# Window attention and a max-of-three feed-forward: later units' scores made with keys stationary, masked as 32x32 blocks, two pairs ahead

## The chip, the cores and the metric

The kernel runs on one core of a Trainium2 chip. The metric is the time of one execution in device microseconds (us). Engines are named as in the profile: PE (TensorE, the matmuls), PEld (TensorE's weight loads), DVE (VectorE), ACT (ScalarE), POOL (GpSimd) and SP (SyncE, whose queue issues the DMAs).

## The reference

Attention over 8 batches, 8 heads, 576 positions and 64 dimensions, then a feed-forward over all 4608 tokens with the maximum of three products:

```python
rel = pos[:, None] - pos[None, :]
mask_plain = (rel >= 0) & (rel < 32)
mask_dil = (rel >= 0) & (rel < 128) & (rel % 4 == 0)     # heads 4 to 7
scores = np.where(mask, q @ k.T / 8, -1e9)
attn = np.exp(scores - scores.max(-1)); attn /= attn.sum(-1) + 1e-9
x = (attn @ v)                                           # as tokens x 512
h = np.maximum(np.maximum(x @ w1, x @ w2), x @ w3)       # 512 -> 768
out = h @ w_out                                          # 768 -> 512
```

All of it is float32. A query sees 32 keys: its own and the 31 before it, in dilated heads those of its own residue modulo 4.

## The kernel before

**Units.** Attention is cut into 64 units: a unit `u` is two heads of one half (288 positions) of a batch; units 0 and 1 of each four are plain heads, 2 and 3 dilated ones. A plain unit has three blocks of 96 queries with 128 keys each, a dilated one four blocks (one residue each) of 72 queries with 104 keys. In a half that begins a sequence (`hf` 0) the first 32 keys of a block don't exist and are left out of the scores.

Units 0 to 11 (below `LEAN`) go through `dense`; their mask is added by a matmul, and their weights of attention are turned by PE (L590). Units 12 to 63 go through `attention` and `behind`, two at a time. For each block and head the scores are a matmul with the queries stationary and the keys streamed (L670): scores come out with queries on partitions. Per block and head, VectorE then adds the mask, scales and takes the maximum in one custom instruction (L702), ScalarE makes the exponential and its sum (L693); where `hf` is 0, POOL clears the missing columns (L728). POOL adds 1e-9 (L738), VectorE takes the reciprocal (L743), POOL multiplies, one instruction for each head (L750), and VectorE turns the result with six transposes of 32x32 blocks, those of the band only (L764), into `PT`. Two units' products with the values (L776, `pv`) follow, and ACT and VectorE round them into the halves `xH` and `xL` that the feed-forward reads.

**Feed-forward.** Nine tiles of 512 tokens. Each has 18 groups of 12 matmuls up (L828: three terms of four, from `wupH`, `wupL`, `xH`, `xL`) in one of two PSUM buffers, whose maximum VectorE keeps in `tmp`, and then four groups of 18 matmuls down (L883). The weights arrive packed and are unpacked on the chip in the start: byte extraction on POOL or VectorE (L420), two joining steps on VectorE (L424, L432), a cast (`wupH`), and a subtraction mostly on POOL (`wupL`, through the helper at L353).

**Order.** Everything is a step of `Plan`. `Plan.order` sets the order of each engine's queue by planned costs, ready times, due times (`deadlines`) and free buffers (`room`), and the program is issued in that order; nothing is reordered at run time. A pair's steps on PE are one step, `products`: the values of the pair that is ready, and behind them the scores of the next pair, so scores run one pair ahead of the values (`unit_pair`, L926). The scores use PSUM buffers "b", six of one bank each; a unit takes two of them for its scores, one for each head, and one for `pv`. While PE has nothing to do in the start, filler matmuls (L962) stand in its queue.

Of the kernel before, what the change touches and what calls it, by code (L numbers as in the profile page):

```python
# [18 lines left out]
WIN, DIL = 32, 4  # L19
# [4 lines left out]
NF = DF // 128  # L24
BLOCK = 256
# [23 lines left out]
def blocks_of(hf, dil):  # L49

    nb, nq, wk = (4, 72, 104) if dil else (3, 96, 128)
    step, out = (104 if dil else 96), []
    for i in range(nb):

        mo = WIN if not hf and (dil or i == 0) else 0
        out.append((nq * i, nq, HALF + step * i + mo, wk - mo, mo))
    return out


def columns(dil):  # L60

    return HALF + (4 * 104 if dil else 320)


class Buf:


    def __init__(self, pool, tag, limit, shape, dtype, name):
        self.pool, self.tag, self.limit = pool, tag, limit
        self.shape, self.dtype, self.name = shape, dtype, name  # L70
        self.users = 0
        self.number = None
        self.end = 0.0
        self.slot = None
        self.t = None

    def take(self):
        if self.t is None and isinstance(self.pool, list):
            self.t = self.pool[self.slot]
        elif self.t is None:  # L80
            self.t = self.pool.tile(self.shape, self.dtype, tag=self.tag, name=self.name, bufs=self.limit)
# [15 lines left out]
class Plan:  # L97
# [48 lines left out]
    def room(self, st, slots):  # L146

        new = [b.tag for b in st.bufs if b.slot is None]
        at = 0.0
        for b in st.bufs:  # L150
            if b.slot is None and b.number is not None and b.number >= self.given.get(b.tag, 0) + new.count(b.tag):
                return 1e9
        for tag in set(new):
            k = new.count(tag)
            at = max(at, sorted(slots[tag])[k - 1][0] if len(slots[tag]) >= k else 1e9)
        return at

    def order(self, fill=None):
# [13 lines left out]
        while len(order) - fills < len(self.steps):  # L172
# [21 lines left out]
            at, _, e, st = best  # L194
            if e == "pe" and st.kind == "ffn":
                fill = None
# [11 lines left out]
            assert at < 1e9, "the steps wait for each other's buffers"  # L208
            for b in st.bufs:
                if b.slot is None:  # L210
                    free_slot = min(slots[b.tag])
                    b.slot = free_slot[1]
                    slots[b.tag].remove(free_slot)
                    self.given[b.tag] = self.given.get(b.tag, 0) + 1
# [21 lines left out]
            for b in st.bufs:  # L236
                b.users -= 1
                b.end = max(b.end, end)
                if not b.users:
                    slots[b.tag].append((b.end + 0.2, b.slot))  # L240
# [21 lines left out]
def tile_dilated_window_attention__then__maxout_ffn(  # L262
# [27 lines left out]
    mask = masks[:, 1]  # L290
# [12 lines left out]
        "k": (4, [128, HALF + 416], F32),  # L303
# [14 lines left out]
    BANKS = {"b": 6, "ffn": 2}  # L318

    def buf(tag, name, shape=None, dtype=None):  # L320
        if tag in BANKS:
            return Buf(ps, tag, BANKS[tag], [128, 512], F32, name)
# [3 lines left out]
        return Buf(work, tag, n, shape or sh, dtype or dt, name)  # L326

# [12 lines left out]

    for t in KEPT["W"]:
        nc.gpsimd.memset(t[:, 768:], 0.0)

    def copy(eng, dst, src):
        if eng == "act":
            nc.scalar.copy(dst, src)  # L346
        elif eng == "pool":
            nc.gpsimd.tensor_scalar(dst, src, 1.0, 1.0, ALU.mult, ALU.mult)
        else:
            nc.vector.tensor_copy(dst, src)  # L350
# [105 lines left out]
    def loads(u, after):  # L456
# [16 lines left out]
            [kload, after[1]],  # L473
# [176 lines left out]
    def attention(u, after):  # L650
# [4 lines left out]
        blocks = blocks_of(hf, dil)  # L655
        nb, nq = len(blocks), blocks[0][1]
        wk = 104 if dil else 128
        kb, kload, v, vload = loads(u, after)
        W, mx, sm = buf("W", f"W{u}"), buf("mx", f"mx{u}"), buf("sm", f"sm{u}")
        banks = [buf("b", f"s{u}_{j}") for j in range(2)]  # L660

        def W3(c0=0):
            return W.t[:, c0 : c0 + 2 * nb * wk].rearrange("p (n k) -> p n k", k=wk)

        def scores():

            for i, (q0, _, k0, nk, mo) in enumerate(blocks):
                for j in range(2):
                    d = slice(64 * j, 64 * j + 64)
                    nc.tensor.matmul(  # L670
                        banks[j].t[:nq, wk * i : wk * i + nk],
                        kb.t[d, q0 : q0 + nq],
                        kb.t[d, k0 : k0 + nk],
                        start=True,
                        stop=True,
                    )

        cost = sum(x[3] / 600 + 0.01 for x in blocks)
        return (scores, cost, [kload], [kb, mx, W, *banks]), (
            lambda s: behind(u, s, blocks, banks, W, W3, mx, sm, v, vload)  # L680
        ), (kload, vload)

    def behind(u, s, blocks, banks, W, W3, mx, sm, v, vload):
# [3 lines left out]
        nb, nq = len(blocks), blocks[0][1]  # L687
        wk = 104 if dil else 128
        expd, cleared = [], None

        def expo(_, n, nk, mo):
            a = W3()[:nq, n, mo : mo + nk]
# [4 lines left out]
        for j in range(2):  # L697
            for i, (*_, nk, mo) in enumerate(blocks):
                n = nb * j + i

                def masked(_, n=n, i=i, j=j, nk=nk, mo=mo):
                    nc.vector.tensor_tensor_reduce(  # L702
                        W3()[:nq, n, mo : mo + nk],
                        banks[j].t[:nq, wk * i : wk * i + nk],
                        mask[:nq, mo : mo + nk],
                        -0.125,
                        3e38,
                        ALU.add,
                        ALU.min,
                        mx.t[:nq, n : n + 1],  # L710
                    )

                t = plan.add({"dve": dve(nk)}, masked, [s], [banks[j], W, mx])
                expd.append(
                    plan.add(
                        {"act": act(nk) + 0.33},
                        lambda _, n=n, nk=nk, mo=mo: expo(_, n, nk, mo),
                        [t],
                        [W, mx, sm],
                    )  # L720
                )


        if not hf:

            def clear(_):
                a = W3() if dil else W.t[:, :768].rearrange("p (j c) -> p j c", j=2)
                nc.gpsimd.memset(a[:, :, :WIN], 0.0)  # L728

            cleared = plan.add({"pool": 0.1 + 0.0008 * (256 if dil else 64)}, clear, [expd[0]], [W])  # L730

        PT = buf(f"PT{dil}", f"PT{u}")
        copied = []

        def eps(e):
            a = sm.t[:nq, : 2 * nb]
            if e == "pool":
                nc.gpsimd.tensor_tensor(a, a, eps_c[:nq].broadcast_to([nq, 2 * nb]), op=ALU.add)  # L738
            else:
                nc.vector.tensor_scalar(a, a, 1e-9, None, ALU.add)  # L740
# [3 lines left out]

        s = plan.add({"pool": 0.22}, eps, expd, [sm])
        r = plan.add({"dve": 0.18}, recip, [s], [sm])
        k0 = WIN if dil and not hf else 0
        normed = []
        for j in range(2):
            n0, n1 = j * nb, (j + 1) * nb  # L750

            def norm(e, n0=n0, n1=n1):
                a = W3()[:nq, n0:n1, k0:]
                tt(e, a, a, sm.t[:nq, n0:n1].unsqueeze(2).broadcast_to([nq, nb, wk - k0]), ALU.mult)

            n = nb * (wk - k0)
            normed.append(plan.add({"pool": 0.13 + 0.00188 * n, "dve": dve(n)}, norm, [r, cleared], [W, sm]))
        for i in range(3):
            for g in (i, i + 1):

                def turn(_, i=i, g=g):
                    c = 32 * g
                    e = max(0, c + 32 - wk)
                    nc.vector.transpose(  # L764
                        PT.t[c : c + 32, : 2 * nb, 32 * i : 32 * i + 32],
                        W3(e)[32 * i : 32 * i + 32, :, c - e : c - e + 32],
                    )

                copied.append(plan.add({"dve": dve(64 * nb)}, turn, normed, [W, PT]))
# [3 lines left out]
        def values():  # L773
            for i, (q0, *_) in enumerate(blocks):
# [151 lines left out]
    def unit_pair(u):  # L926
# [8 lines left out]
        s, xs = products([x for _, x in made], [x[1] for x in pair])  # L935
        for (x, _), r in zip(made, xs):
            x_of[divmod(x, NPAIR)] = r(waits(x // NPAIR))
        made = [(x, rest(s)) for x, _, rest in pair]

    u = t0 = 0  # L940
    for n in TILES:
        plan.kind = "a"
        while HALF * (u // NPAIR) < t0 + n:

            for p in range(NPAIR):
# [3 lines left out]
                elif u == LEAN and p == 0:  # L949
                    unit_pair(u)  # L950
                if u >= LEAN and p % 2:
                    unit_pair(u + 1)
# [17 lines left out]
def _layouts(q, k, v, moe_w1, moe_w2, moe_w3, moe_w_out):  # L970
# [13 lines left out]
    for hf in range(2):  # L984
# [4 lines left out]
        lay[f"qk_d{hf}"] = np.concatenate(x, axis=2).transpose(0, 1, 3, 2).reshape(B, 2, 128, -1)  # L989
# [34 lines left out]
```

## Time and profile before

| | us |
|---|---|
| median of 3 runs | 723.75 (721.61 to 724.37) |
| profiled execution, its own time | 724.2 |
| its span, first to last instruction | 722.3 |

The page lists busy time by engine, the granted clock of PE in 40 slices, and groups of instructions with busy time (overlaps counted once) and the mean duration of one. Two groups that the prediction doesn't show: ScalarE's exponentials (L693) are 134.1 us busy in 364 instructions, and the feed-forward's four groups of 648 matmuls on PE are 676.6 us busy. The mean granted clock is 0.990.

### The profile page before, as it was taken

What the parts mean: (1) busy time and instruction counts of PE and PEld (TensorE: products, weight loads), DVE (VectorE), ACT (ScalarE), POOL (GpSimd) and SP (SyncE); (2) the same over time, 40 slices, a digit from 0 to 9 for tenths busy, and PEclk for the clock granted to TensorE, in tenths of its full rate; (3) what the DMA queues carried; (4) which work ended last, traced back from release to release, by engine and by line L of the source; (5) the groups of instructions that cost most, each with busy time, mean ns of one, the idle gap of its engine ahead of it and who ended that gap; (6) DMA issues with size and microseconds to landing.
All of it is one profiled execution on the core that took longest, in us unless ns stands there. A gap on an engine that the chain in (4) does not pass through costs nothing.

```text
span 722.3 us, 12780 instructions
## 1 busy us (share of the span) xinstructions
PE 712.2 (99%) x4534; PEld 578.2 (80%) x4539; DVE 371.7 (51%) x1456; ACT 294.5 (41%) x1101; POOL 231.9 (32%) x328
## 2 busy tenths in 40 slices
PE   8899999999999999999999999999999999999997
PEld 4577878888888888888888888888888888888886
DVE  5978966556556554655456555655555511101110
ACT  4866763334444444444434334434343411111111
POOL 3888762233223332322222222332223301200110
PEclk9969999999999999999999999999999999999999
DMA  8991532211222223212321222112220010000001
GB/s 262 344 325 49 185 101 93 75 32 58 89 89 63 59 78 102 63 59 64 103 77 60 63 76 92 49 37 80 87 64 25 15 44 0 1 29 30 1 0 59
DMA packets 31232, 57.45 MB, mean 80 GB/s; under 512 B 3008, under 2 KB 11200, under 8 KB 31168
## 3 DMA queue, kind: packets, MB, share of 16 engines
q1 hardware_dynamic: 31168, 56.64, 24.4%
q8 instruction: 36, 0.59, 0.3%
q14 instruction: 28, 0.23, 0.1%
HBM read 47.19 MB, written 9.44 MB: 78 GB/s over the span
## 4 chain that ended last, share of the span: by engine, by line
PE 95%; POOL 2%; DVE 1%; DMA 1%; issue 0%; SPq 0%; ACT 0%; POOLq 0%; ACTq 0%; DVEq 0%
PE u L828 62%; PE d L883 21%; PE s L670 5%; PE pv L776 4%; PE s L509 1%; DMA st<-in_w_up_dram 1%; POOL W L353 1%; PE pt L590 1%; PE pv L604 1%; PE idle L962 0%; POOL wupL L353 0%; PE s L504 0%; DVE mx L527 0%; DVE sm L544 0%; POOL c L420 0%
## 5 line engine op out<-in xcount | busy, mean ns | idle before, releaser
L353 DVE TENSOR_TENSOR tmp<-u,tmp 128x512 f32<-128x512 f32 x108 | 74.7, 691 | 206.6 <-PE u L828 190.0
L828 PE MATMUL u<-xL,wupH 128*128 128x512 f32 x648 | 176.3, 394 | 0.0
L828 PE MATMUL u<-xH,wupH 128*128 128x512 f32 x648 | 175.4, 393 | 0.0
L828 PE MATMUL u<-xH,wupL 128*128 128x512 f32 x648 | 174.1, 390 | 0.0
L883 PE MATMUL d<-wdn,h 128*128 128x512 f32 x648 | 150.8, 391 | 0.0
L353 POOL TENSOR_TENSOR h<-tmp,h 128x512 fp32r<-128x512 f32 x54 | 69.7, 1290 | 244.6 <-ACT h L346 244.6
L693 ACT ACTIVATE W<-W,mx 96x128 f32<-96x128 f32 (+3 forms) x364 | 134.1, 371 | 27.0 <-DVE mx L702 25.9
L828 PEld LDWEIGHTS u<-xH,wupL 128*128 128x128 f32 x648 | 121.4, 188 | 25.9
L883 PEld LDWEIGHTS d<-wdn,h 128*128 128x128 f32 x648 | 121.1, 188 | 26.3
L828 PEld LDWEIGHTS u<-xH,wupH 128*128 128x128 f32 x648 | 121.4, 189 | 25.8
L828 PEld LDWEIGHTS u<-xL,wupH 128*128 128x128 f32 x648 | 120.9, 189 | 26.4
L764 DVE STREAM_TRANSPOSE PT<-W 32x192 f32<-32x192 f32 (+1 forms) x312 | 124.7, 400 | 32.3 <-POOL W L353 28.1
L346 ACT CAST h<-tmp 128x512 fp32r<-128x512 f32 x54 | 33.4, 619 | 208.9 <-DVE tmp L353 208.8
L353 POOL TENSOR_TENSOR W<-W,sm 96x384 f32<-96x384 f32 (+3 forms) x125 | 99.2, 812 | 45.2 <-DVE sm L743 40.3
L702 DVE CUSTOM_DVE_ANT_0 W<-s,masks 96x128 f32<-96x128 f32 (+3 forms) x364 | 70.1, 257 | 52.6 <-PE s L670 52.6
L693 ACT ACTIVATION_READ_ACCUMULATOR W<-W,mx 72x1 f32 (+1 forms) x364 | 68.6, 189 | 0.0
L738 POOL TENSOR_TENSOR sm<-sm,small_c 96x6 f32<-96x6 f32 (+1 forms) x52 | 10.3, 198 | 166.3 <-ACT W L693 166.1
L346 ACT COPY tmp<-u 128x512 f32<-128x512 f32 x54 | 31.7, 587 | 67.9 <-PE u L828 51.2
L346 ACT COPY o<-d 128x512 f32<-128x512 f32 x36 | 21.1, 587 | 82.3 <-PE d L883 75.3
L670 PE MATMUL s<-k 64*96 64x128 f32 (+3 forms) x728 | 38.7, 254 | 0.0
L670 PEld LDWEIGHTS s<-k 64*72 64x72 f32 (+1 forms) x728 | 33.7, 149 | 2.8 <-ACT tmp L346 0.4
L776 PEld LDWEIGHTS pv<-PT,v 104*64 104x64 f32 (+1 forms) x728 | 27.2, 137 | 9.2 <-issue 8.8
(56 smaller groups left out, 410.9 us busy)
## 6 DMA issues: line engine op xcount, KB each, us to landing
k<-in_qk_d_dram SPq DMA_DIRECT2D x32, 352.0 KB, 3.0
k<-in_qk_p_dram SPq DMA_DIRECT2D x32, 304.0 KB, 3.2
st<-in_w_up_dram SPq DMA_DIRECT2D x18, 512.0 KB, 10.4
out_dram<-o SPq DMA_DIRECT2D x36, 256.0 KB, 2.0
v<-in_v_d_dram SPq DMA_DIRECT2D x32, 208.0 KB
v<-in_v_p_dram SPq DMA_DIRECT2D x32, 192.0 KB, 6.1
st<-in_w_dn_dram SPq DMA_DIRECT2D x12, 256.0 KB, 2.6
```

The costliest lines, as they stand in the source:

```text
L346: nc.scalar.copy(dst, src)
L353: (nc.vector if eng == "dve" else nc.gpsimd).tensor_tensor(dst, a, b, op=op)
L509: nc.tensor.matmul(S3(j)[:nq, i], kb.t[d, nq * i : nq * i + nq], kb.t[d, k0 : k0 + wk], start=False, stop=True, skip_group_check=True,)
L590: nc.tensor.transpose(bank.t[:wk, nq * i : nq * i + nq], W3()[:nq, nb * j + i], ident[:nq, :nq])
L670: nc.tensor.matmul(banks[j].t[:nq, wk * i : wk * i + nk], kb.t[d, q0 : q0 + nq], kb.t[d, k0 : k0 + nk], start=True, stop=True,)
L693: nc.scalar.activation(a, a, AF.Exp, bias=mx.t[:nq, n : n + 1], scale=-1.0, accum_out=sm.t[:nq, n : n + 1])
L702: nc.vector.tensor_tensor_reduce(W3()[:nq, n, mo : mo + nk], banks[j].t[:nq, wk * i : wk * i + nk], mask[:nq, mo : mo + nk], -0.125, 3e38, ...
L738: nc.gpsimd.tensor_tensor(a, a, eps_c[:nq].broadcast_to([nq, 2 * nb]), op=ALU.add)
L764: nc.vector.transpose(PT.t[c : c + 32, : 2 * nb, 32 * i : 32 * i + 32], W3(e)[32 * i : 32 * i + 32, :, c - e : c - e + 32],)
L776: nc.tensor.matmul(pv.t[64 * j : 64 * j + 64, q0 : q0 + nq], v.t[:wk, j, i, :], PT.t[:wk, nb * j + i, :nq], start=True, stop=True,)
L828: nc.tensor.matmul(sums(bank), wt[:, 3 * f + g, c, :], moving(xL if xz else xH, c), start=(m == 0 and c == 0), stop=(m == 2 and c == 3),)
L883: nc.tensor.matmul(bank.t, hs[f].t[:, hz, s0 : s0 + 128], wdn[f].t[:, wz], start=(f == 0 and m == 0), stop=(f == NF - 1 and m == 2),)
```

## The change

Scores of units 12 to 63 are made with the keys stationary (128 columns) and the queries streamed (96 or 72 columns; the last block streams 96 in every unit, for which the dilated loads are 24 columns longer), so that keys are on partitions. Both heads' scores lie in two neighbouring PSUM banks (`span=2`; the six banks "b" are now one tile). VectorE turns them back with six transposes of 32x32 blocks, of the band only, into `W`, which then holds 64 columns for each block and head instead of 128 or 104. The mask (`narrow`, bf16) is added by POOL, VectorE takes one maximum over all blocks, POOL scales it, the exponentials read 64 columns, and one multiplication on POOL normalises both heads. No columns are cleared any more. Scores run two pairs ahead of the values (`AHEAD`). In the dense units, the values' load no longer waits for the keys' load.

```diff
             lambda _: nc.sync.dma_start(out=v.t[:nk, :, :nb, :], in_=vsrc),
-            [kload, after[1]],
+            [after[1]] if u < LEAN else [kload, after[1]],
...
-            for i, (q0, _, k0, nk, mo) in enumerate(blocks):
+            for i in range(nb):
+                k0 = HALF + k_step * i
+                n = 96 if i == nb - 1 else nq
                 for j in range(2):
                     d = slice(64 * j, 64 * j + 64)
                     nc.tensor.matmul(
-                        banks[j].t[:nq, wk * i : wk * i + nk],
-                        kb.t[d, q0 : q0 + nq],
-                        kb.t[d, k0 : k0 + nk],
+                        sT.t[:, j, nq * i : nq * i + n],
+                        kb.t[d, k0 : k0 + 128],
+                        kb.t[d, nq * i : nq * i + n],
...
+        for i in range(3):
+            for g in range(2):
+                def turn_in(_, i=i, g=g):
+                    r = slice(32 * i, 32 * i + 32)
+                    c = 32 * (i + g)
+                    src = sT.t[c : c + 32, :, 32 * i : 32 * i + nq * (nb - 1) + 32]
+                    src = bass.AP(
+                        src.tensor, src.offset, [list(src.ap[0]), list(src.ap[1]), [nq * src.ap[2][0], nb], [src.ap[2][0], 32]]
+                    )
+                    dst = W3(r)[:, :, 32 * g : 32 * g + 32].rearrange("p (j n) k -> p j n k", j=2)
+                    nc.vector.transpose(dst, src)
+                turned.append(plan.add({"dve": dve(64 * nb)}, turn_in, [s], [sT, W]))
...
-                    nc.vector.tensor_tensor_reduce(
-                        W3()[:nq, n, mo : mo + nk],
-                        banks[j].t[:nq, wk * i : wk * i + nk],
-                        mask[:nq, mo : mo + nk],
...
+        t = plan.add({"pool": pool(nw)}, masked, turned, [W])
+        t = plan.add({"dve": dve(nw)}, most, [t], [W, mx])
+        t = plan.add({"pool": 0.22}, eighth, [t], [mx])
...
-                a, a, AF.Exp, bias=mx.t[:nq, n : n + 1], scale=-1.0, accum_out=sm.t[:nq, n : n + 1]
+                a, a, AF.Exp, bias=mx.t[:nq, n : n + 1], scale=0.125, accum_out=sm.t[:nq, n : n + 1]
...
+        s = plan.add({"pool": 0.13 + 0.00188 * nw, "dve": dve2(2 * nw)}, norm, [s], [W, sm])
...
-        s, xs = products([x for _, x in made], [x[1] for x in pair])
+        ready = made.pop(0) if len(made) == AHEAD else []
+        s, xs = products([x for _, x in ready], [x[1] for x in pair])
...
-        made = [(x, rest(s)) for x, _, rest in pair]
+        made.append([(x, rest(s)) for x, _, rest in pair])
```

PE's queue at the values of units 18 and 19 (`pv18`, `pv19`), in the second feed-forward tile, before; `s20_0` and `s20_1` are the scores of unit 20's two heads, `k20` its queries and keys, and the size is that of the output:

```order
L776 MATMUL pv18_1974<-PT1_0_86,v18_1632 64x72 x8
L776 MATMUL pv19_1975<-PT1_1_87,v19_1670 64x72 x8
L670 MATMUL s20_0_1977<-k20_1626 96x128
L670 MATMUL s20_1_1978<-k20_1626 96x128
L670 MATMUL s20_0_1977<-k20_1626 96x128
L670 MATMUL s20_1_1978<-k20_1626 96x128
L670 MATMUL s20_0_1977<-k20_1626 96x128
L670 MATMUL s20_1_1978<-k20_1626 96x128
```

The same place in the changed kernel, where all scores and values lie in the tile `banks`:

```order
L794 MATMUL banks_89<-PT1_0_87,v18_1631 64x72 x8
L794 MATMUL banks_89<-PT1_1_88,v19_1658 64x72 x8
L690 MATMUL banks_89<-k22_1625 128x72 x6
L690 MATMUL banks_89<-k22_1625 128x96 x2
L690 MATMUL banks_89<-k23_1655 128x72 x6
L690 MATMUL banks_89<-k23_1655 128x96 x2
```

Behind the values of 18 and 19 now stand the scores of 22 and 23, not of 20 and 21, and the outputs have 128 partitions of keys and 72 or 96 columns of queries. Both programs have 364 such matmuls.

SP's queue in the start before, from the third key load to the third packed weight (`st2`); `k` are queries and keys, `v` values:

```order
L465 DMA k2_106<-in_qk_d0_dram 128x704
L465 DMA k3_108<-in_qk_d0_dram 128x704
L438 DMA st0_110<-in_w_up_dram 128x512
L438 DMA st1_112<-in_w_up_dram 128x512
L472 DMA v0_133<-in_v_p0_dram 128x2x192
L465 DMA k4_147<-in_qk_p1_dram 128x608
L465 DMA k5_167<-in_qk_p1_dram 128x608
L472 DMA v1_173<-in_v_p0_dram 128x2x192
L465 DMA k6_177<-in_qk_d1_dram 128x704
L472 DMA v2_204<-in_v_d0_dram 104x512
L472 DMA v3_209<-in_v_d0_dram 104x512
L438 DMA st2_217<-in_w_up_dram 128x512
```

And in the changed kernel, again up to `st2`:

```order
L495 DMA v1_118<-in_v_p0_dram 128x2x192
L495 DMA v5_120<-in_v_p1_dram 128x2x192
L495 DMA v2_139<-in_v_d0_dram 104x512
L495 DMA v3_141<-in_v_d0_dram 104x512
L495 DMA v4_143<-in_v_p1_dram 128x2x192
L488 DMA k4_155<-in_qk_p1_dram 128x608
L488 DMA k5_171<-in_qk_p1_dram 128x608
L461 DMA st0_179<-in_w_up_dram 128x512
L488 DMA k6_203<-in_qk_d1_dram 128x728
L461 DMA st1_210<-in_w_up_dram 128x512
L488 DMA k7_231<-in_qk_d1_dram 128x728
L461 DMA st2_243<-in_w_up_dram 128x512
```

The six value loads `v0` to `v5` and the key loads `k4` and `k5` moved ahead of the first weight, `st0` (`v0` stands two rows ahead of the first one shown, right behind `k2`).

POOL's queue in the start before, up to the last normalisation (`W<-W,sm`) that the first feed-forward tile needs, that of unit 7 (`W_80`):

```order
L353 TENSOR_TENSOR W_81<-W_81,sm_406 96x384 x2
L353 TENSOR_TENSOR W_83<-W_83,sm_316 96x416 x2
L353 TENSOR_TENSOR wupL<-c_313,wupH 128x512
L353 TENSOR_TENSOR wupL<-c_385,wupH 128x512
L353 TENSOR_TENSOR W_82<-W_82,sm_446 96x416 x2
L420 TENSOR_SCALAR c_567<-st_336 128x512
L420 TENSOR_SCALAR c_595<-st_356 128x512
L353 TENSOR_TENSOR W_80<-W_80,sm_562 96x416 x2
```

And in the changed kernel, up to the same normalisation (`W_81` there):

```order
L376 TENSOR_TENSOR W_82<-W_82,sm_376 96x384 x2
L376 TENSOR_TENSOR W_84<-W_84,sm_312 96x416 x2
L376 TENSOR_TENSOR wupL<-c_289,wupH 128x512
L376 TENSOR_TENSOR W_83<-W_83,sm_406 96x416 x2
L443 TENSOR_SCALAR c_525<-st_292 128x512
L376 TENSOR_TENSOR W_81<-W_81,sm_492 96x416 x2
```

From the queue's head to this row there were seven byte extractions (`c<-st`) and four subtractions (`wupL`); now there are five and two, and one cast to `wupH`.

More of the change, by code (lines that the diff above doesn't have):

```diff
@@ L24 @@
 NF = DF // 128
+PAD = 24
+AHEAD = 2
 BLOCK = 256
@@ L46, with __init__ @@
 WEIGHT_PACE, WEIGHT_SLACK, WEIGHT_LEAD = 0.3, 3.188, 0.8
[L49 to L57, printed above, removed]
 def columns(dil):
-    return HALF + (4 * 104 if dil else 320)
+    return HALF + (4 * 104 + PAD if dil else 320)
 class Buf:
-    def __init__(self, pool, tag, limit, shape, dtype, name):
+    def __init__(self, pool, tag, limit, shape, dtype, name, span=1):
+        self.span = span
         self.pool, self.tag, self.limit = pool, tag, limit
@@ L194, in order @@
             at, _, e, st = best
+            assert at < 1e9, "the steps wait for each other's buffers"
             if e == "pe" and st.kind == "ffn":
@@ L207, in order @@
                 fills += 1
-            assert at < 1e9, "the steps wait for each other's buffers"
-            for b in st.bufs:
+            self.now = at
+            for b in sorted(st.bufs, key=lambda b: -b.span):
                 if b.slot is None:
-                    free_slot = min(slots[b.tag])
-                    b.slot = free_slot[1]
-                    slots[b.tag].remove(free_slot)
+                    b.slot = self.pick(b, slots[b.tag])
                     self.given[b.tag] = self.given.get(b.tag, 0) + 1
@@ L239, in order @@
                 if not b.users:
-                    slots[b.tag].append((b.end + 0.2, b.slot))
+                    slots[b.tag] += [(b.end + 0.2, b.slot + i) for i in range(b.span)]
             for n in st.next:
@@ L289, in tile_dilated_window_attention__then__maxout_ffn @@
     masks = const.tile([128, 4, 128], BF16, name="masks")
-    mask = masks[:, 1]
+    narrow = const.tile([96, 4, 64], BF16, name="narrow")
     wupH = const.tile([128, 3 * NF, 4, 128], F32R, name="wupH")
@@ L316, in tile_dilated_window_attention__then__maxout_ffn, with buf @@
     }
[L318 to L322, printed above, removed]
+    NB = 6
+    banks_b = ps.tile([128, NB, 512], F32, name="banks", bufs=1)
+    BANKS = [banks_b[:, i] for i in range(NB)] + [banks_b[:, i : i + 2] for i in range(0, NB, 2)]
+    def buf(tag, name, shape=None, dtype=None, span=1):
+        if tag == "b":
+            return Buf(BANKS, tag, NB, None, None, name, span)
+        if tag == "ffn":
+            return Buf(ps, tag, 2, [128, 512], F32, name)
         if tag in KEPT:
@@ L676, in scores, with behind @@
                     )
-        cost = sum(x[3] / 600 + 0.01 for x in blocks)
-        return (scores, cost, [kload], [kb, mx, W, *banks]), (
-            lambda s: behind(u, s, blocks, banks, W, W3, mx, sm, v, vload)
+        cost = nb * (nq / 600 + 0.03) + 0.03
+        return (scores, cost, [kload], [kb, mx, W, sT]), (
+            lambda s: behind(u, s, nb, nq, sT, W, mx, sm, v, vload)
         ), (kload, vload)
-    def behind(u, s, blocks, banks, W, W3, mx, sm, v, vload):
+    def behind(u, s, nb, nq, sT, W, mx, sm, v, vload):
         half, p = divmod(u, NPAIR)
@@ L745, in behind @@
         s = plan.add({"pool": 0.22}, eps, expd, [sm])
[L746 to L757, printed above, removed]
+        s = plan.add({"dve": 0.18}, recip, [s], [sm])
```

137 lines of the change are left out of this document (77 added, 60 removed).

## The prediction

> **What bounds the kernel now.** I read the page first: busy time of each engine, and the chain of work that ended last.
>
> ```profile
> PE 712.2 (99%) x4534; PEld 578.2 (80%) x4539; DVE 371.7 (51%) x1456; ACT 294.5 (41%) x1101; POOL 231.9 (32%) x328
> PE 95%; POOL 2%; DVE 1%; DMA 1%; issue 0%; SPq 0%; ACT 0%; POOLq 0%; ACTq 0%; DVEq 0%
> ```
>
> TensorE is busy for 99% of the span, and the chain runs through it for 95%. A busy PE need not be a PE at its peak, so the next views are its waits and a table by stage (columns: stretch, its length; PE, PEld, DVE, ACT and POOL busy; granted clock of PE, DMA share, GB/s).
>
> ```profile
> PE idle L962 <- DVE masks L339: 3.0, 1, 3.0
> PE pt L590 <- POOL W L353: 1.5, 3, 0.9
> ...
> 20.00:40.00 20.00, 17.83 (x199) 12.12 (x199) 18.86 (x48) 16.30 (x57) 18.91 (x23) 0.88 1.03 354
> 40.00:60.00 20.00, 19.78 (x97) 15.89 (x99) 14.96 (x28) 15.14 (x35) 16.77 (x17) 0.78 0.62 215
> 60.00:80.00 20.00, 19.85 (x135) 15.27 (x134) 18.33 (x41) 13.02 (x43) 15.82 (x19) 1.00 0.38 116
> 80.00:100.00 20.00, 20.00 (x138) 16.11 (x138) 18.83 (x67) 13.84 (x49) 15.80 (x25) 1.00 0.40 132
> 100.00:150.00 50.00, 50.00 (x365) 40.91 (x364) 27.39 (x141) 23.58 (x102) 15.31 (x25) 1.00 0.30 92
> ```
>
> The two longest waits of PE are 3.0 and 1.5 us, both in the start. From 80 us on PE waits for nobody, and from 100 us on VectorE is busy for 27.4 of 50 us. So in the steady part **only the length of PE's own stream counts**. Making scores two pairs ahead gives PE time that it does not lack: I cost it at nothing there. What is left is what the scores take on PE, and what the new order does to the start.
>
> **The scores on PE.** One call makes a pair's scores as one burst. The chain, in order of time, lists each burst (start, length, what):
>
> ```profile
> 274.05 1.39 PE s L670 x24
> ...
> 292.50 1.19 PE s L670 x32
> ...
> 312.31 1.48 PE s L670 x24
> ...
> 331.48 1.58 PE s L670 x32
> ```
>
> These are the four kinds: plain heads (24 records) in a half that begins a sequence and in the other, dilated heads (32 records) in the same two. Units 12 to 63 are 26 pairs: 6 of 1.39, 7 of 1.48, 6 of 1.19, 7 of 1.58, in sum 36.9 us.
>
> The 12 (16) matmuls of a unit pair and of its two heads become 24 (32) records, and the two heads' go side by side (their loads come in pairs, x2 and x4 below), so a burst is 12 steps for plain and 16 for dilated heads. Before, a step loads 96 or 72 columns of queries and streams 72 to 128 columns of keys. Now each step loads **128 columns of keys** and streams 96 or 72 columns of queries. Streaming shrinks, loading grows, and the question is which one sets the step. The weight loads at the head of three bursts show it. I cut the timeline right behind the first load (or pair of loads) and behind the second; the second length minus the first is the time from one load to the next.
>
> ```profile
> 292.43 0.14 PEld L670 LDWEIGHTS s<-k 64*72 64x72 f32 x2
> 292.43 0.21 PEld L670 LDWEIGHTS s<-k 64*72 64x72 f32 x4
> 312.24 0.16 PEld L670 LDWEIGHTS s<-k 64*96 64x96 f32 x2
> 312.24 0.25 PEld L670 LDWEIGHTS s<-k 64*96 64x96 f32 x4
> 313.72 0.19 PEld L828 LDWEIGHTS u<-xL,wupH 128*128 128x128 f32 x1
> 313.72 0.30 PEld L828 LDWEIGHTS u<-xL,wupH 128*128 128x128 f32 x2
> 313.72 0.53 PEld L828 LDWEIGHTS u<-xL,wupH 128*128 128x128 f32 x3
> ```
>
> 72 columns: 0.07 us; 96: 0.09; 128: 0.11. The time grows with the columns, in 64 rows as in 128. The third load of the last group comes 0.23 us behind the second, though a load takes 0.11: it waits until the matmul before it has taken up its weights. So one load runs ahead and no more, and a step cannot be shorter than its load. A 128-column load gives a step of 0.11 us, whatever is streamed.
>
> That is also the step of the 1.48 us burst, which streams 128 columns in each of 12 steps (1.48 / 12 is 0.12 with its ends). So a plain pair becomes about 1.50 (first load 0.02 longer than that of 96 columns), and a dilated one, four steps more, 1.50 + 4 x 0.11 = 1.94. Sum: 13 x 1.50 + 13 x 1.94 = 44.7, that is **+7.8 us**. With steps of 0.107 to 0.112 it is +7.2 to +8.6. Dilated pairs carry it: 16 loads of 0.11 instead of 0.07.
>
> One row speaks against this:
>
> ```profile
> 84.91 0.50 PEld L590 LDWEIGHTS pt<-ident,W 72*104 72x104 f32 x7
> ```
>
> Seven loads of 104 columns in 0.50 us is under 0.07 each. But these belong to transposes by an identity, another kind of matmul; the nearest row for the new loads is the old scores' own, same tensor and rows, and it gives 0.09 for 96. I take 0.11 and keep the other as a rival.
>
> The Trainium skill, "TensorE: Matmul & The Clock Gate", section "Weight-path perf modes — Fast Weight Load (FWL) and DoubleRow", says that loads go several times faster when they hold 128 weights and the type is not FP32. The new loads reach just that width, and they are FP32, so by this page the sum stays; if it applied, the first rival's sum would hold. The 0.11 us for 128 columns above is in line with no fast load in this trace.
>
> **The other engines.** For a plain unit:
>
> ```profile
> L764 DVE STREAM_TRANSPOSE PT<-W 32x192 f32<-32x192 f32 x156 | 57.4, 368 | 19.2 <-POOL W L353 17.0
> L702 DVE CUSTOM_DVE_ANT_0 W<-s,masks 96x128 f32<-96x128 f32 x132 | 29.3, 282 | 28.3 <-PE s L670 28.3
> L702 DVE DVE_READ_ACCUMULATOR2_ANT mx<- 96x1 f32 x156 | 12.3, 79 | 0.0
> L527 DVE TENSOR_REDUCE mx<-s 96x3 f32<-96x384 f32 x12 | 6.1, 541 | 5.3 <-PE s L509 5.3
> L353 POOL TENSOR_TENSOR W<-W,sm 96x384 f32<-96x384 f32 x62 | 50.1, 826 | 16.6 <-DVE sm L743 12.0 <-ACT W L541 3.9 <-DVE sm L575 0.4
> ```
>
> VectorE loses six fused mask-and-maximum steps (29.3 / 132 + 0.08 = 0.30 each, 1.8) and gains six transposes (6 x 0.37 = 2.2) and a maximum (0.5): +0.9 us. A transpose out of PSUM is not shown; by the two row kinds here it lies between 0.28 and 0.54, that is +0.4 to +2.0 a unit, and I take 0.37. POOL gives up one of two normalisations (0.83) and gets a mask addition and a scaling; the addition isn't shown, I take 0.83 and bound it by 0.4 and 1.7. ScalarE's exponentials narrow to 64 columns. Five units in 50 us make VectorE 27.4 + 4.5 = 32 of 50 (37 at the worst), and POOL's 15.3 leaves room for all of it: hidden behind PE. The longer way from scores to values has two pair intervals instead of one, so it costs nothing either. Without this cover it would be 0.9 us a unit, 47 us.
>
> **The start.** Feed-forward begins when eight dense units are done, and POOL is last in front of it:
>
> ```profile
> 12.08 6.52 DMA st<-in_w_up_dram
> ...
> 28.27 3.47 POOL W L353 x4
> ...
> 39.13 1.27 POOL wupL L353
> ...
> 45.23 15.52 PE u L828 x60
> ...
> L353 POOL TENSOR_TENSOR wupL<-c,wupH 128x512 fp32r<-128x512 f32 x18 | 23.6, 1324 | 2.9 <-ACT wupH L346 2.4
> L420 POOL TENSOR_SCALAR c<-st 128x512 uint32<-128x512 uint8 x15 | 10.1, 670 | 9.0 <-DMA st<-in_w_up_dram 7.9
> ```
>
> In the new order two byte extractions (0.67) and two subtractions (1.32) fewer stand on POOL ahead of the eighth unit's last normalisation, and one cast more (some 0.7): 3.3 us less. Against it, the first weight load moves behind six value loads and two key loads on SP's queue, and it was a weight load that the chain waited for until 18.6. The work put off is still due before the weights' own groups. Bounds: -5 (POOL's 3.3, and VectorE also has two weights less in front) to +2 (the third weight comes some 0.8 MB later, at the 354 GB/s of 20 to 40 us). I take **-1.0**, between the ends since the engines, 94% busy from 20 to 40 us, only trade places of work.
>
> Sum against the profiled execution's own 724.2: 724.2 + 7.8 - 1.0 = 731.0. The median of the runs shown is 0.45 lower, so I predict **730.5**.
>
> **Rivals.**
> 1. *Streaming sets the step* (ends on the other side). If the new loads ran at the transposes' speed or were hidden, steps would be those of streaming, 96 and 72 parts in 128 of 0.11, 0.083 and 0.063 us; with 0.2 for the ends plain pairs take about 1.20 and dilated ones 1.28: 32.2, or -4.7 instead of +7.8, and 718; with 0.08 for every load, plain 1.22 and dilated 1.50, -1.5 and 721. It decides as soon as a load of 128 columns takes under some 0.09. For it: the row of transposes. Against: three widths on one line. The Trainium skill, same page, section "Back-to-back issue gap", lets the isolated gap follow the streamed columns alone; by it this rival would come true, and the loads quoted above speak against it.
> 2. *VectorE becomes late in the first tile.* From 60 to 100 us it has 2.8 us free, and four units' new transposes and maxima (4 x 2.7) want in. If they push the copies that free PSUM, PE waits 3 to 9 us: 734 to 740. Against: their values are now due one pair later.
> 3. *The start gets longer*, because the first weights come late and PE's clock, 0.78 from 40 to 60 us, stays down longer: +3 to +6 on the forecast, 734 to 737.
>
> **How the numbers follow.** Forecast 0.70, rivals 0.13, 0.10 and 0.07. The low end is 724.2 + 7.2 - 5 - 0.45 = 726, the high end 724.2 + 8.6 + 2 + 3.5 - 0.45 = 738, which takes in rival 3 and half of rival 2; left out are rival 1 and the rest of rival 2, under 0.2. A measurement of this kernel can tell about 0.5% from no change, which is 720.1 to 727.4. Faster takes most of rival 1: 0.09; same its rest and the forecast's low tail: 0.12; slower 0.79.
>
> **What would show it.** The chain should give the score line 44 to 46 us, with bursts of 1.50 and 1.94 and none below 1.4; the score loads should follow each other by 0.11. PE should have no wait behind 60 us, VectorE some 50 us more in all, and the first up-projection should begin between 40 and 47 us. Dilated bursts of 1.2 to 1.3 would prove the load argument wrong; a PE idle for VectorE would make it rival 2.

## The result, and the profile after

| | us |
|---|---|
| changed kernel, median of 4 runs | 830.13 (829.03 to 831.12) |
| kernel before, beside it on the same chip | 723.77 (721.61 to 724.37) |
| ratio | 1.1475, 95% interval 1.1445 to 1.1506 |
| profiled execution's span | 829.0 (before 722.3) |

The change costs 106 us, where 7 were forecast. The page of the changed kernel, busy time and then the chain that ended last:

```profile
PE 750.7 (91%) x4539; PEld 600.2 (72%) x4539; DVE 465.4 (56%) x1066; ACT 292.6 (35%) x1122; POOL 264.3 (32%) x365
PE 73%; DVE 3%; ACT 0%; issue 0%; ACTq 0%; DVEq 0%
```

The page's chain reaches back only to 187 us, so TensorE's 73% are nearly all of the 77% of the span that it covers, and it says nothing of what lies ahead of that. The table by stage does (columns as in the prediction: stretch, length, PE, PEld, DVE, ACT, POOL, granted clock, DMA share, GB/s):

```profile
20.00:40.00 20.00, 10.18 (x54) 5.60 (x53) 7.96 (x20) 5.90 (x23) 4.51 (x6) 0.59 0.37 120
40.00:60.00 20.00, 11.83 (x77) 7.29 (x76) 5.98 (x15) 5.94 (x20) 6.66 (x9) 0.50 0.56 210
60.00:80.00 20.00, 9.62 (x71) 6.24 (x69) 9.79 (x22) 7.41 (x27) 7.96 (x8) 0.67 0.30 105
80.00:100.00 20.00, 10.33 (x68) 6.22 (x70) 5.64 (x10) 6.89 (x15) 6.66 (x7) 0.50 0.17 54
```

From 20 to 40 us the kernel before had PE, VectorE and GpSimd busy for 17.83, 18.86 and 18.91 us; now it is 10.18, 7.96 and 4.51. **TensorE is busy for about half of this time and every other engine for less.** That is not the picture of one engine that is too slow: it is the picture of engines that take turns. The first up-projection shows the delay (timeline, start and length first):

```profile
103.12 1.65 PE L846 MATMUL u<-xH,wupH 128*128 128x512 f32 x3
```

It came at 45.2 us before, so 57.9 us are lost by then. The second feed-forward tile's first matmul (the 217th record on this line) comes at 228.7 us, before at 129.9: 98.8 us are lost by there. From it to the end there are 600.3 us, before 592.4: +7.9, of which 5.7 are the scores (PE is busy with them for 39.8 us there, before for 34.1). The other 98.8 us all lie in front.

Which operations take turns is read from PE's longest waits (what waited, for what: us in total, times, longest). On PE, L527 are the dense units' scores, L613 the turning of their weights and L627 their values; L550 is VectorE's maximum over dense scores, L575 ScalarE's exponential, and L436 and L447 belong to the unpacking of the feed-forward's weights:

```profile
PE banks L613 <- ACT PT L348: 8.3, 4, 2.5
PE banks L527 <- DVE mx L550: 8.1, 3, 4.6
PE banks L613 <- ACT W L575: 7.8, 4, 3.0
PE banks L613 <- DVE banks L447: 4.3, 3, 2.3
PE banks L627 <- ACT banks L436: 3.5, 3, 1.4
```

and from the timeline at 61 us (start, length; in brackets the idle time before it and what ended it):

```profile
60.81 0.19 DVE L556 TENSOR_SCALAR mx<-mx 96x4 f32<-96x4 f32 x2
61.05 0.34 ACT L575 ACTIVATE W<-banks,mx 96x104 f32<-96x104 f32 x1 [1.45 <-DVE mx L556]
...
61.52 0.59 DVE L550 TENSOR_REDUCE mx<-banks 96x4 f32<-96x416 f32 x1 [0.51 <-ACT W L575]
62.14 0.34 ACT L575 ACTIVATE W<-banks,mx 96x104 f32<-96x104 f32 x1 [0.65 <-DVE mx L550]
...
62.61 0.59 DVE L550 TENSOR_REDUCE mx<-banks 96x4 f32<-96x416 f32 x1 [0.50 <-ACT W L575]
...
63.23 0.34 ACT L575 ACTIVATE W<-banks,mx 96x104 f32<-96x104 f32 x1 [0.65 <-DVE mx L550]
...
64.03 0.70 DVE L447 SCALAR_TENSOR_TENSOR banks<-banks,c 128x512 uint32<-128x512 uint32 x1 [0.72 <-ACT W L575]
```

ScalarE's exponentials (L575) and VectorE's maxima (L550) alternate, each starting when the other ends. No data passes between them: a maximum is scaled by L556 before an exponential uses it, and no L556 lies between 61.52 and 64.03. Nor does the joining of weight bytes at 64.03 need an exponential. All they have in common is that each touches some bank of the tile `banks`, and not the same one: in the built program the exponentials of these rows read bank 0, the two maxima banks 4 and 3, and the joining step works on bank 5, and each waits for the other engine's end. In that whole program ScalarE and VectorE have 207 waits for each other's instructions on this tile, and in 199 of them the instruction waited for touches only *other* banks.

**Theory:** the change put six PSUM banks, six tiles before, into one tile so that a unit can hold two neighbours (`span=2`), and accesses of different engines to different banks of one tile are now ordered one after the other. **Rivals:** the start's new load order, VectorE's longer work, or scores that cost more than forecast.

### The profile page after: what moved, and what is told of

Same layout as the page of the kernel before. It is cut to its first block, busy times and chain, and to the rows that moved or that the text cites. A ratio compares the mean times of both kernels' runs of the same rounds, so it can differ in the third digit from the quotient of the medians.

```text
span 829.0 us, 12420 instructions
## 1 busy us (share of the span) xinstructions
PE 750.7 (91%) x4539; PEld 600.2 (72%) x4539; DVE 465.4 (56%) x1066; ACT 292.6 (35%) x1122; POOL 264.3 (32%) x365
## 4 chain that ended last, share of the span: by engine, by line
PE 73%; DVE 3%; ACT 0%; issue 0%; ACTq 0%; DVEq 0%
PE u L846 46%; PE d L901 18%; PE banks L690 5%; PE banks L794 4%; DVE W L726 1%; DVE PT L781 0%; DVE tmp L376 0%; DVE mx L740 0%; ACT xH L348 0%; DVE banks L447 0%; DVE c L455 0%; DVE xL L376 0%; ACT banks L436 0%; PE banks L627 0%; ACT o L348 0%
## 5 line engine op out<-in xcount | busy, mean ns | idle before, releaser
L846 PE MATMUL u<-xH,wupH 128*128 128x512 f32 x648 | 179.4, 399 | 6.9 <-DVE tmp L376 3.2
L846 PE MATMUL u<-xL,wupH 128*128 128x512 f32 x648 | 178.9, 399 | 0.0
L754 ACT ACTIVATE W<-W,mx 72x64 f32<-72x64 f32 (+1 forms) x364 | 121.7, 337 | 76.3 <-POOL mx L746 76.3
L726 DVE STREAM_TRANSPOSE W<-banks 32x192 f32<-32x192 f32 (+1 forms) x312 | 128.3, 411 | 25.5 <-ACT xH L348 9.8
L846 PEld LDWEIGHTS u<-xL,wupH 128*128 128x128 f32 x648 | 123.1, 192 | 26.7 <-issue 0.3
L376 POOL TENSOR_TENSOR W<-W,sm 96x384 f32<-96x384 f32 (+2 forms) x74 | 67.0, 910 | 104.1 <-DVE sm L598 51.7
L376 POOL TENSOR_TENSOR W<-W,narrow 96x384 f32<-96x384 f32 (+1 forms) x52 | 54.1, 1040 | 121.5 <-DVE W L726 121.5
L690 PE MATMUL banks<-k 64*128 64x96 f32 (+1 forms) x728 | 46.9, 277 | 2.9 <-ACT wdn L348 1.6
L690 PEld LDWEIGHTS banks<-k 64*128 64x128 f32 x728 | 42.7, 187 | 6.0 <-issue 2.0
L348 ACT CAST xH<-banks 128x288 fp32r<-128x288 f32 (+6 forms) x74 | 24.7, 363 | 57.9 <-DVE W L726 20.0
```

Source lines behind the costliest of these rows:

```text
L376: (nc.vector if eng == "dve" else nc.gpsimd).tensor_tensor(dst, a, b, op=op)
L690: nc.tensor.matmul(sT.t[:, j, nq * i : nq * i + n], kb.t[d, k0 : k0 + 128], kb.t[d, nq * i : nq * i + n], start=True, stop=True,)
L726: nc.vector.transpose(dst, src)
L754: nc.scalar.activation(a, a, AF.Exp, bias=mx.t[:nq, n : n + 1], scale=0.125, accum_out=sm.t[:nq, n : n + 1])
L846: nc.tensor.matmul(sums(bank), wt[:, 3 * f + g, c, :], moving(xL if xz else xH, c), start=(m == 0 and c == 0), stop=(m == 2 and c == 3),)
```

## The experiments

All medians stand beside runs of the kernel before on the same chip (722.9 to 723.4 us); three rounds each unless one run is named.

**e1: the changed kernel with three two-bank tiles**, and the same order on every engine:

```diff
-    banks_b = ps.tile([128, NB, 512], F32, name="banks", bufs=1)
-    BANKS = [banks_b[:, i] for i in range(NB)] + [banks_b[:, i : i + 2] for i in range(0, NB, 2)]
+    PAIRS = [ps.tile([128, 2, 512], F32, name=f"banks{i}", bufs=1) for i in range(NB // 2)]
+    BANKS = [PAIRS[i // 2][:, i % 2] for i in range(NB)] + [t[:, :] for t in PAIRS]
```

> The changed kernel with its six PSUM banks as three tiles of two banks instead of one tile of six; every engine's queue holds the same instructions in the same order. Theory 'one tile' (in the start, instructions on different banks wait for each other because all banks are one tile): most of the 106 us go, 728 to 760 us, the first up-projection begins before 70 us. Rival 'order' (the new order of loads and steps makes the start long): 825 to 835 us. Rival 'longer chain' (turning scores on VectorE and masking on POOL are too slow in the start): also 825 to 835 us. In all of them the score bursts stay at 1.51 and 1.96 us.

Measured: 747.62 us (745.35 to 750.24), ratio 1.0334 (1.0303 to 1.0365): 82.5 us come back. The engines are at work in the start again:

```profile
20.00:40.00 20.00, 15.60 (x152) 10.53 (x155) 16.43 (x42) 14.10 (x52) 14.14 (x17) 0.93 0.93 329
40.00:60.00 20.00, 17.69 (x117) 12.84 (x117) 14.08 (x25) 14.45 (x29) 14.33 (x17) 0.73 0.58 186
```

**e2: the kernel before with its six buffers in one tile**, nothing else changed:

```diff
+    banks_b = ps.tile([128, 6, 512], F32, name="banks", bufs=1)
+    ONE = [banks_b[:, i] for i in range(6)]
...
+        if tag == "b":
+            return Buf(ONE, tag, 6, None, None, name)
```

> The kernel before with its six score buffers as slices of one tile of six banks; same instructions, same order. Theory 'one tile': it becomes much slower too, 790 to 840 us, with all engines under half busy in the first 100 us. Rivals 'order' and 'longer chain': it stays at 720 to 730 us, since neither is in this kernel.

Measured, one run: 813.05 us, 89.6 over the kernel before, with the same empty start:

```profile
20.00:40.00 20.00, 10.84 (x52) 5.86 (x51) 8.13 (x20) 7.28 (x25) 6.22 (x8) 0.59 0.41 133
60.00:80.00 20.00, 7.73 (x52) 5.04 (x50) 5.76 (x16) 6.17 (x24) 8.76 (x10) 0.61 0.28 95
```

Taken away, the one tile gives back 82 us; put alone into the kernel before, it costs 90. That settles the main cause.

**e3 and e4: what sets the step of a score** (on e1, one run each). e3 loads 64 of the 128 key columns (the scores of the other keys aren't made), e4 streams 32 query columns of 72 or 96 (the scores of the others aren't made):

```diff
-                        sT.t[:, j, nq * i : nq * i + n],
-                        kb.t[d, k0 : k0 + 128],
+                        sT.t[:64, j, nq * i : nq * i + n],
+                        kb.t[d, k0 : k0 + 64],
```

```diff
-                        sT.t[:, j, nq * i : nq * i + n],
+                        sT.t[:, j, nq * i : nq * i + 32],
...
-                        kb.t[d, nq * i : nq * i + n],
+                        kb.t[d, nq * i : nq * i + 32],
```

> e1_pairs with only 64 of the 128 key columns loaded for the scores of units 12 to 63 (the other scores are not computed). If the load sets the step, steps fall to those of streaming, 0.083 us for 96 and 0.063 for 72 columns: bursts of about 1.20 and 1.28 us, and 8 to 10 us less than e1_pairs. If streaming or something else sets it, the bursts stay at 1.51 and 1.96.

> e1_pairs with only 32 query columns streamed in each score matmul of units 12 to 63 (the other scores are not computed). If the 128-column load sets the step, the bursts stay within 0.1 us of 1.51 and 1.96 (only the last stream is shorter). If streaming sets it, they fall below 1.0.

Measured: 733.43 and 744.96 us against e1's 747.62. The chain lists the bursts (start, length). In e1:

```profile
218.13 1.96 PE banks L690 x32
236.00 1.51 PE banks L690 x24
```

with 64 columns loaded:

```profile
214.38 1.23 PE banks L690 x32
231.52 1.14 PE banks L690 x24
```

and with 32 streamed:

```profile
216.16 1.91 PE banks L690 x32
233.98 1.46 PE banks L690 x24
```

Streaming a third of the columns moves a burst by 0.05 us; loading half of them moves the 16 steps of a dilated burst by 0.73, or 0.046 a step. The load sets the step, as the prediction argued; rival 1 falls, and the gap of an isolated matmul that the prediction cites for it isn't the step of such a burst. Over 13 dilated and 13 plain bursts e3's loads save 14.3 us, which is what its one run shows (14.2); 8 to 10 had been expected.

**e5: six one-bank tiles**, so that no bank shares its tile. A unit's heads then have a tile each, and VectorE turns them back with 12 transposes of half the width:

```diff
-    banks_b = ps.tile([128, NB, 512], F32, name="banks", bufs=1)
+    BANKS = [ps.tile([128, 512], F32, name=f"bank{i}", bufs=1) for i in range(NB)]
...
-        sT = buf("b", f"s{u}", span=2)
+        sT = [buf("b", f"s{u}_{j}") for j in range(2)]
...
+        for j, i, g in [(j, i, g) for j in range(2) for i in range(3) for g in range(2)]:
```

> The change with six tiles of one bank each: a unit's two heads have their scores in two tiles, and VectorE turns them back one head at a time, in twelve transposes of half the width instead of six. If the rest of e1_pairs (747.6 against a sum of 731) comes from neighbours in a tile that still wait for each other: 728 to 737 us. If it comes from the new order of loads and steps or from VectorE's longer work in the start: 743 to 752 us (the twelve transposes add work to VectorE).

Measured: 747.64 us (747.01 to 748.78), a miss: no faster than e1. The start is full and the first up-projection comes at 42.4 us, but PE now stands in the second feed-forward tile (a stretch, then PE's waits for the values' rounding):

```profile
125.00:150.00 25.00, 18.29 (x122) 14.24 (x119) 20.01 (x61) 6.74 (x32) 5.57 (x10) 0.82 0.35 111
```

```profile
PE u L840 <- ACT xH L347: 3.9, 1, 3.9
PE u L840 <- DVE xL L375: 2.5, 1, 2.5
```

This version has 515 us of VectorE work where e1 has 462, so it trades the neighbour's wait for more of VectorE. It can't divide the two; e13 and e15 below try each alone.

**e6, e8: the order of the value loads.** e6 is e5 with the rule of before (its edit is shown), e8 the kernel before with the changed rule (the reverse):

```diff
-            [after[1]] if u < LEAN else [kload, after[1]],
+            [kload, after[1]],
```

> e5_heads with the value loads of the dense units waiting for the key loads again, as before. If the first weights' late loads cost time in the start: 3 to 12 us less than e5_heads. If the engines, not the loads, set the start: within 2 us of it.

> The kernel before with the changed rule for the value loads of the dense units alone. If the order of loads sets the start: 3 to 12 us slower than before. If not: 721 to 726 us.

Measured: e6 743.16 (741.62 to 743.41), e8 728.25 (727.67 to 729.44), ratio 1.0070 (1.0055 to 1.0085). In both the changed order costs some 5 us, but not by a later start: the first up-projection comes earlier with it, at 42.4 us in e5 (e6: 49.1) and at 43.2 in e8 (before: 45.2). In e5 PE then stands longer at the head of the second tile (the 6.4 us above; in e6 one wait of 1.6). In e8 the second tile's first matmul comes 0.7 us later than before, and nearly all of the loss is in the down-projection's matmuls, in the kernel before and in e8:

```profile
L883 PE MATMUL d<-wdn,h 128*128 128x512 f32 x648 | 150.8, 391 | 0.0
L883 PE MATMUL d<-wdn,h 128*128 128x512 f32 x648 | 155.1, 398 | 0.0
```

These 4.3 us are as much as the two profiled spans differ (726.5 less 722.3). What makes the same matmuls longer is not shown. Of the built programs, only those of e8 and of e14, which has the same 155.1 us, place the buffers `wdn` at multiples of 64 bytes; all others have them 32 bytes off. No run tests whether that is the reason.

**e7: e5 with scores only one pair ahead** (`AHEAD = 1`).

> e5_heads with scores one pair ahead of the values again. If four units' turning in the first feed-forward tile crowds VectorE: 4 to 12 us less than e5_heads. If the longer lead neither costs nor brings anything: within 2 us. If the longer lead hides VectorE's longer chain: slower, by 5 us or more.

Measured: 808.09 us (806.98 to 809.43), 60 over e5. PE's longest wait:

```profile
PE bank L788 <- DVE PT L775: 52.0, 8, 14.2
```

The lead of two pairs is what hides the longer chain; without it PE waits for the turned weights of attention, in eight waits of up to 14.2 us.

**e9: e1 with the old value loads.** Same edit as e6.

> The changed kernel with three two-bank tiles and with the dense units' value loads waiting for the key loads as before. If the load order costs the start 4.5 to 5 us whatever the rest is (743.2 against 747.6 with one-bank tiles, 728.3 against 723.2 in the kernel before), this gives 747.6 - 5 = 742 to 744. If two heads in one tile and the load order cost the same waiting time, so that one hides the other, it stays at 746 to 748.

Measured: 755.42 us (751.53 to 756.26), ratio 1.0440 (1.0410 to 1.0470): neither theory. With two-bank tiles the *old* order is 8 us slower. So load order and neighbours are not independent, and 8 us of e1's gain on the changed kernel hang on the changed order: its first up-projection comes at 52.0 us, that of e9 at 61.6.

**e10: the kernel before with scores two pairs ahead.**

```diff
-        s, xs = products([x for _, x in made], [x[1] for x in pair])
+        ready = made.pop(0) if len(made) == AHEAD else []
+        s, xs = products([x for _, x in ready], [x[1] for x in pair])
```

> The kernel before with its scores two pairs ahead and nothing else. If the lead is worth nothing where VectorE's chain is short (TensorE waits for nobody there from 80 us on), 722 to 726. If holding two pairs' scores and weights of attention at once costs buffers that the start or the first tiles need, 728 to 740.

Measured: 723.37 us (10 runs), ratio 1.0004 (0.9994 to 1.0014): nothing, as forecast.

**e11: e9 without the maximum; e12: e9 with 104 key columns loaded in dilated units.**

```diff
-        t = plan.add({"dve": dve(nw)}, most, [t], [W, mx])
-        t = plan.add({"pool": 0.22}, eighth, [t], [mx])
...
-                a, a, AF.Exp, bias=mx.t[:nq, n : n + 1], scale=0.125, accum_out=sm.t[:nq, n : n + 1]
+                a, a, AF.Exp, bias=zero[:nq], scale=0.125, accum_out=sm.t[:nq, n : n + 1]
```

```diff
-                        kb.t[d, k0 : k0 + 128],
+                        kb.t[d, k0 : k0 + (104 if dil else 128)],
```

> The kernel with two-bank tiles and the old load order, and with no maximum in units 12 to 63: neither VectorE's reduction nor GpSimd's scaling of it is made, and the exponentials take a bias of zero. This takes some 0.6 us of VectorE out of each unit and two steps out of its chain. If what is left over the score term (743 - 731 = 12 us) is VectorE's lateness in the first two tiles, it gives back 4 to 8 us: 735 to 739. If VectorE's load isn't the cause, it gives 741 to 744.

> The kernel with two-bank tiles and the old load order, and dilated units' score loads of 104 key columns instead of 128 (the 24 columns belong to no query of their block). If the load sets the step, a dilated burst goes from 1.94 to 1.56 to 1.62 (16 x 0.021 to 0.024 less), 13 of them: -4 to -5 us, so 738 to 740 if the two-bank kernel with the old load order gives 743. If streaming or a fixed gap sets it, no change.

Measured: e11 757.54 us (754.88 to 758.01), a miss: no gain over e9's 755.42, though VectorE has 26 us less to do (431.9 against 457.5 up to 720 us). The planner orders the start anew, and the first up-projection comes at 63.5 us instead of 61.6; a change of cost in the plan moves this start by as much as what was to be measured. e12: 750.08 us (747.13 to 751.87), 5.3 under e9; the expected total was missed because e9 was; the difference lies near the 4 to 5 expected, though the bursts, 1.64 us where 1.56 to 1.62 had been expected, give only 13 x 0.32 = 4.2 of it. Its bursts:

```profile
220.68 1.64 PE banks L690 x32
238.23 1.51 PE banks L690 x24
```

24 columns less in 16 loads take 0.32 us off the 1.96 of a dilated burst, 0.020 a step. The Trainium skill, "TensorE: Matmul & The Clock Gate", section "LDWEIGHTS (loading the stationary operand)", gives a load's time as its columns over 1.2, in ns; an estimate by it is 0.020 us for 24 columns, and these bursts agree. For e3's 64 columns the same estimate is 0.053, where 0.046 a step were measured.

**e13, e14, e15: the two remaining costs, each alone in the kernel before.** e13 has its six buffers as halves of three two-bank tiles, with its order unchanged; e14 is e13 with the changed value loads; e15 has one-bank tiles and the old scores, two pairs ahead, with more VectorE work in each later unit:

```diff
+    PAIRS = [ps.tile([128, 2, 512], F32, name=f"banks{i}", bufs=1) for i in range(3)]
+    HALVES = [PAIRS[i // 2][:, i % 2] for i in range(6)]
```

```diff
+        def dummy(_):
+            nc.vector.transpose(junk[:, 1, : 64 * nb], junk[:, 0, : 64 * nb])
+        first = [plan.add({"dve": dve(64 * nb)}, dummy, [s], [W]) for _ in range(4 if dil else 5)]
...
-                t = plan.add({"dve": dve(nk)}, masked, [s], [banks[j], W, mx])
+                t = plan.add({"dve": dve(nk)}, masked, [s, *first], [banks[j], W, mx])
```

> The kernel before with its six score buffers as halves of three two-bank tiles, same order on every engine. If sharing a tile with one neighbour makes engines wait for each other in the start, 735 to 745, with the first up-projection later than 45 us and its neighbours' waits in the start; if only a tile of many banks does harm, 722 to 726.

> The same with the changed load order of the dense units' values. If load order and sharing add up, 5 more than with the pairs alone. In the changed kernel with pairs the changed load order was the faster one by 8 (747.6 against 755.4); if that comes of the dense units alone, this run is faster than the one with the pairs alone.

> The kernel before, scores two pairs ahead, and between the scores and the masks of each later unit five (plain) or four (dilated) transposes more on VectorE, of a tile that nothing else uses: some 93 us of VectorE in all, as in the changed kernel, with one-bank tiles and the old scores. If VectorE's load and the longer chain make the first two feed-forward tiles late, 730 to 740; if they hide behind TensorE, 722 to 726.

Measured: e13 737.02 us (736.45 to 737.43), ratio 1.0195 (1.0179 to 1.0211); e14 738.78 (738.45 to 741.31); e15 732.75 (732.01 to 734.77), ratio 1.0142 (1.0117 to 1.0167). One neighbour costs 14.1 us, in the start (e13, where before had PE at 17.83 and 19.78, VectorE at 18.86 and 14.96):

```profile
20.00:40.00 20.00, 16.74 (x135) 10.14 (x133) 11.56 (x33) 12.11 (x45) 11.15 (x14) 0.74 0.82 289
40.00:60.00 20.00, 15.71 (x134) 11.64 (x137) 15.74 (x32) 14.81 (x32) 15.61 (x17) 0.83 0.72 232
```

VectorE's load costs 9.9, and elsewhere: the first up-projection comes at 42.6 us, even earlier than the 45.2 of before, but PE then stands at the head of the second tile, waiting for rounded values (e15, one stretch, and the waits; 5.5 us of them, 3.8 and 1.7, are in this stretch):

```profile
125.00:150.00 25.00, 19.45 (x124) 14.97 (x124) 18.31 (x90) 10.61 (x49) 4.46 (x9) 0.80 0.21 68
```

```profile
PE u L835 <- DVE xL L356: 4.6, 2, 3.8
PE u L835 <- ACT xH L349: 1.7, 1, 1.7
```

The granted clock in this stretch is 0.80, in the kernel before 1.00. The added work loads VectorE and also makes the chain from scores to values longer; e15 doesn't divide these two.

Neighbours 14.1, VectorE 9.9 and the scores' 8 make 32.0 over the kernel before; e9, which has these three and the old load order, is 32.1 over it. But the traces do not bear this sum out. From the second tile's first matmul to the end e9 takes 598.1 us and e10, with the old scores and the same lead, 591.1; the longer scores alone (39.7 us of PE there against 32.8) make this difference, and PE has no wait there. So e15's 9.9 us are not in e9. Up to that matmul e9 loses 21.6 us (151.5 against 129.9), where e13 loses 13.0. So that the three add up to e9's total is chance. No version tried beats the kernel before.

## Why the prediction was wrong, point by point

**The scores on PE: right.** Forecast were bursts of 1.50 and 1.94 us; the chain of the changed kernel shows

```profile
246.10 1.51 PE banks L690 x24
264.47 1.96 PE banks L690 x32
```

13 of each make 45.1 us instead of 36.9, +8.2 where +7.8 was predicted. The argument from the load, against the row of transposes, held (e3, e4, e12).

**The failed step: "the engines ... only trade places of work", and with it the start term of -1.0** (bounds -5 to +2). The prediction compared what stands in each queue and what it lasts. The one tile has no term in it: which instructions the new tile orders after each other was not asked. On each engine the order is what the planner made, but between the engines there are waits that no data calls for: +89.6 us when only the tile is changed (e2), -82.5 us when it is cut in three (e1). The sign it named, a first up-projection between 40 and 47 us, is missed by 56. The wait to look for was in the change itself: `banks_b = ps.tile([128, NB, 512], ...)`, and `banks_89` in every row of the order.

The Trainium skill, "PSUM — Partial Sum Buffer", section "PSUM bank collisions raise a hardware error", asks that engines be kept apart for each bank and 32 partitions, and says that accesses of two engines to different banks run clean. By it the waits between banks were not needed, and the start of the kernel before, whose six buffers lie in six tiles, agrees: there TensorE, VectorE and ScalarE were busy side by side for 17.83, 18.86 and 16.30 of 20 us. The program waited all the same.

**"Hidden behind PE": right in the changed kernel, but not everywhere.** From the second tile's first matmul on, PE has no wait above 0.4 us in the changed kernel and none above 0.2 in e1 (busy for 200.00 us from 200 to 400). Where the start is early, VectorE's work is not free at the second tile's head: PE stands there for 5.5 us in e15, which is 9.9 us slower in all, and for 6.4 in e5. That is rival 2, a tile later than it said, in versions that the forecast was not made for. The size of VectorE's work was wrong: 93.7 us more (465.4 less 371.7) where some 50 were forecast. The groups of after, and of before:

```profile
L726 DVE STREAM_TRANSPOSE W<-banks 32x192 f32<-32x192 f32 (+1 forms) x312 | 128.3, 411 | 25.5 <-ACT xH L348 9.8 <-PE banks L690 5.3 <-PE banks L627 2.0
L740 DVE TENSOR_REDUCE mx<-W 96x6 f32<-96x384 f32 (+1 forms) x52 | 31.0, 612 | 3.6 <-POOL W L376 2.8
```

```profile
L702 DVE CUSTOM_DVE_ANT_0 W<-s,masks 96x128 f32<-96x128 f32 (+3 forms) x364 | 70.1, 257 | 52.6 <-PE s L670 52.6
L702 DVE DVE_READ_ACCUMULATOR2_ANT mx<- 72x1 f32 (+1 forms) x364 | 28.7, 79 | 0.0
```

What came in is 128.3 + 31.0 = 159.3 us, each piece near its forecast. What went out is 70.1, not 70.1 + 28.7: the prediction added the 0.08 us of each accumulator read, but they lie beside the custom instructions, and the two rows together keep VectorE busy for 70.4 us. So 88.9 of the 93.7 us are this exchange.

**The longer chain costs nothing with two pairs ahead: right, and the cover is real.** e10 shows that the lead itself is free, e7 that without it 60 us are lost. The 47 us named for that case are near by chance: they were 0.9 us for each unit, and e7 loses its time in eight long waits.

**Rival 3, the first weights late: not seen.** In all four pairs of profiled executions the changed load order brings the first up-projection forward, by 2.0 us (e8 against before), 6.7 (e5 against e6), 4.9 (e14 against e13) and 9.6 (e1 against e9). So the sign of the start term was right for the queues that it compared. What is left of this at the end is another matter: the totals are 5.0, 4.5 and 1.8 us longer and 7.8 shorter. The 5.0 and 4.5 lie within this rival's "+3 to +6", but in e8's down-projection and at e5's second tile, not in a longer start.

**Two loose readings that change nothing.** Seven loads in 0.50 us are 0.071 each, not under 0.07. And the "94% busy" holds for VectorE and GpSimd; TensorE was at 89% and ScalarE at 82%.

**What stays open:** why only e1 keeps to the end what the changed load order gains in the start, why taking VectorE's maximum away gained nothing in e11, what e9 loses in front beyond e13's 13.0 us, and why e8's down-projection is slower. In e11 and e9 the planner or the loads changed the order of a start in which neighbours wait for each other; which wait tips it was not found.

## What to carry to other kernels

When a change merges buffers into one tile, ask which instructions of different engines the merged tile now orders, even if they touch different banks and only read; TensorE about half busy and all others less at the same time, waiting for each other across operations that share no data, is its mark. Make a tile no larger than what one instruction must address as a whole. And bound a start by trying its order as it is: a change of load order that looked free moved the first up-projection forward by 2 to 10 us here and the total by -8 to +5.

## What the runs showed of the hardware and had not been expected

The turn-back transposes out of PSUM take about as long as those out of SBUF (378 ns for 32x192 and 445 for 32x256, against 368 and 435). And in a start full of gaps PE was also granted less clock: in the four stretches from 20 to 100 us, with PE busy for 9.62 to 11.83 of 20 us, the granted clock was 0.50 to 0.67 in the changed kernel, before 0.78 to 1.00.
